# Delta-rule attention and a hardswish MLP in one kernel: two weight-conversion steps change their places in a hand-written order around the first join

## The chip, the cores and the metric

One core of one Trainium2 chip. The metric is the time of one execution of the program on the device, in microseconds, median of several runs. The core has five engines that run side by side, each working through its own queue in order: TensorE (PE in the profile), VectorE (DVE), ScalarE (ACT), GpSimd (POOL) and SyncE (SP, which here issues DMAs). Where one needs what another makes, it waits on a semaphore, and everything behind it in its queue waits too.

## The reference

```python
# q, k, v: (4, 8, 768, 48), beta: (4, 8, 768), all f32
k_n = k / (norm(k, axis=-1) + 1e-6)
for t in range(768):
    y[:, :, t] = q_t @ state
    v_old = state^T k_t
    state = state + beta_t * outer(k_t, v_t - v_old)
x = y.transpose(0, 2, 1, 3).reshape(3072, 384)
h = x @ w_in                              # w_in (384, 2048)
g = h * clip(h + 3, 0, 6) / 6
out = g @ w_out                           # w_out (2048, 384)
```

The weights come in as 64-bit floats, which the kernel turns into 32-bit floats itself.

## The kernel before

**Attention in chunks.** The 768 tokens are cut into 24 chunks t of 32; the four batches lie side by side on the 128 partitions. A chunk needs the inverse X of a 32x32 triangular matrix for each batch and head. Chunk 0 gets it by products on TensorE. Chunks 1 to 4 form the first group: their inverse is a substitution on VectorE for all four at once, with pairs of small operations (L730 product, L735 subtraction), that does both 16x16 halves of each matrix; a memset (L740) and a transpose back (L473) end it. Then each chunk has a *join* that makes the off-diagonal quarter from the two halves: a GpSimd memset, a transpose on VectorE (L694), 64 small products on TensorE (L684, the "first products"), an addition and a second transpose on VectorE (L698, L702), 64 more products (L684, the "second products"), and a ScalarE copy into X (L710).

The chunk's own chain is: products with the state (L806), R on VectorE (two L901, one L909: values less what the state holds), pz = X R on TensorE (L827), the copy Z of it on ScalarE (L927), the output py (L827), the state's update su (L938, applied by L956 on VectorE), and y (L843 on ScalarE, L819 and L863 on VectorE), which TensorE turns (yt, L873) and ScalarE copies to xT (L877).

**The MLP beside it.** Two chunks make a block of 256 tokens. For the very first chunk the up projection runs alone as 16 blocks of w_in columns, f0 to f15, each three accumulated f32 matmuls on TensorE (L994, six PE instructions in the profile). Each is followed by a relu on ScalarE (L1001) and a "second half" on VectorE (L1004) that multiplies it with the PSUM result and thereby frees the PSUM bank. The second chunk has 16 more of its own. These banks come from a ring of four, which the transposes and the products of the attention share. Which result a new one waits for is decided when the program is made: it takes the bank whose last result is read first.

**The weights.** They are 16 pieces, eight of w_in and eight of w_out, numbered from 0. A piece is loaded raw; ScalarE makes its power-of-two scale in four dependent passes over a half-buffer of `spare` (L356, `es[i % 2]`: even pieces use one half, odd pieces the other); VectorE converts in three steps: integer bits of the high word (L378), the low word added (L383), and the product with the scale into its home (L389). The first step and the second go through one common buffer. Column blocks f12 and f13 need piece 6, f14 and f15 piece 7. The program asserts, word by word, that the scale of piece i is begun only after piece i-2 is converted.

**The order.** Up to chunk 5 the order of all this is written out by hand in the string ORDER; a word advances a generator by one step, `*n` n times. The words that matter here:

- `c`: one conversion step (L378, L383, L389 in turn). `a`: one scale pass (L356).
- `i1`: one step of the first group's substitution. `x1`: one step of chunk 1's join. `h1`: one step of chunk 1's chain. `y0`, `y1`: one step of the output of chunk 0 or 1.
- `ua`: one up-projection block of the first chunk (`ub` of the second). `ra`, `rb`: its relu. `ga`, `gb`: its second half.
- `n5`: norms of later keys (a square on ScalarE L407, a reduction on VectorE L413). `k`, `v`, `q`, `w`: DMA issues on SyncE for keys, values, queries and raw weights.

A word gives the engine's queue its next instruction, so the place of a word fixes what stands in front of it on its own engine, and nothing else.

Of the kernel before, what the change touches and what calls it, by code (L numbers as in the profile page):

```python
# [24 lines left out]
n2 k*2 a x0 m2 p1 c*2 p1 n2*3 b1 q b0 s p1 x0 q w x0 n2 q*2 c*3 x0 n4 k p1 k p2*2 x0*2 a*2 c a*2 q*3  # L25
a*2 w v p3*2 q x0 q n4 p2*2 c p2 v c n4*2 a*3 z v n4 c a m3 v c p2 n4*2 q p2 k c b2 h0 c h0 w a*2 h0
p4*2 a*2 m4 p3 q*4 h0 q k w p4*2 c*5 v*2 p3 k p3*3 k*2 p4*2 v*2 p4 m6 k a w a w i1*3 k i1*7 a i1*2 a
i1*2 v i1*2 k b3 k y0 c y0*3 ua*2 ra*2 i1*3 w v ga v a*3 i1*2 ua i1 h1 i1 q w ua ra ua i1 ra*2 ga i1
k ua a*2 ra ga i1 ga ua ra ua ra i1 ga i1*4 ua ga n5 x1*2 k x1 c a ra v a*2 ga x2 k*2 ga*2 ua*2 x1
ra*2 x1*2 ua h1*2 n5 k ga c ra ga*2 h1 c y1*2 ua ra w ga ua ra x2 n5 ga y1*2 ua ra ga h1 v*3 n5*2 k  # L30
y1*2 ua a ra x2 ub*2 a n5 rb*2 h1 x3 ga c*2 v W a h2 y2 gb ub rb gb x2 gb ub*2 n5*2 b4 rb n5 x2*2 h2
gb rb gb m5 a n5*2 y2 ub rb gb v c q*2 v q*5 n5 ub n5 rb gb h2 c h2 q ub y2 h2 y2 rb ub p5 b5 rb
gb*2 a*2 x3 p5 ub y2*2 k p5*2 h2 rb h3 p5 gb h3 ub*2 q rb gb rb gb ub a x3 p6 v c x4 x3 rb gb ub p7
# [1531 lines left out]
```

## Time and profile before

| what | value |
|---|---|
| median of 3 runs | 664.41 us (663.94 to 665.17) |
| the profiled execution | 662.06 us, its span (first to last instruction) 660.3 us |
| TensorE busy | 632.5 us, 96% of the span |
| VectorE busy | 499.2 us, 76% |
| ScalarE busy | 282.3 us, 43% |
| GpSimd busy | 225.1 us, 34% |
| granted TensorE clock, mean | 0.997 of full speed |

Busy shares are means over stages that differ. In the first 60 us the attention is set up, weights stream in, and all engines take turns at holding up the others; later TensorE works nearly without a break. The part that the change touches lies between 53 and 67 us. There, VectorE, ScalarE and TensorE hand work to each other within fractions of a microsecond, so the timelines, which list instructions in order of time, say more than the shares do. In a timeline line the columns are start, length, engine, line of the kernel, operation, output and inputs, shape, count, and in brackets how long the engine had been idle and what ended the wait. A start can overlap the end of the instruction in front of it by about 0.1 us, since an engine takes up the next one while the last drains.

### The profile page before, as it was taken

The numbers are of one execution on the slowest core, as the hardware profiler recorded it, in microseconds if no ns is written. First come the engines' busy times: TensorE is split into PE (matmuls) and PEld (weight loads), VectorE is DVE, ScalarE is ACT, GpSimd is POOL, SyncE is SP. The second block draws the span as 40 slices with busy tenths as digits, with TensorE's granted clock in tenths as the row PEclk, the third lists the DMA queues.
The fourth block names the chain that finished last, engine by engine and source line by source line (L and its number), as shares of the span: only waits on it lengthen the run. The fifth ranks groups of instructions, "written<-read, shape, count | busy, mean of one in ns | idle before, by whom it ended". The sixth has DMA issues, their size and how long they took to land.

```text
span 660.3 us, 26640 instructions
## 1 busy us (share of the span) xinstructions
PE 632.5 (96%) x11640; PEld 569.2 (86%) x11640; DVE 499.2 (76%) x1170; ACT 282.3 (43%) x548; POOL 225.1 (34%) x352
## 2 busy tenths in 40 slices
PE   2768999999999999999999999999999999999997
PEld 2658987776689989999999999999999999999997
DVE  5899877798657988758988848979658998456354
ACT  5887689332243154154154244244244144153250
POOL 6531022003661353553254354164051242331430
PEclk9998999999999999999999999999999999999999
DMA  7888346202040030041030030020020020000000
GB/s 174 204 198 235 77 102 164 51 25 43 9 87 18 3 74 3 3 90 22 3 74 3 2 74 3 2 63 2 3 50 2 3 49 3 23 18 2 26 1 24
DMA packets 88692, 33.28 MB, mean 50 GB/s; under 512 B 80224, under 2 KB 83424, under 8 KB 88576
## 3 DMA queue, kind: packets, MB, share of 16 engines
q1 hardware_dynamic: 88224, 31.29, 20.8%
q8 instruction: 91, 1.49, 0.9%
q10 hardware_dynamic: 352, 0.30, 0.2%
q14 instruction: 25, 0.20, 0.1%
HBM read 26.84 MB, written 4.72 MB: 48 GB/s over the span
## 4 chain that ended last, share of the span: by engine, by line
PE 91%; DVE 3%; DMA 2%; SPq 1%; ACT 1%; issue 1%; DVEq 0%
PE po L1226 28%; PE ph L1066 27%; PE ph L994 9%; PE po L1162 6%; PE ks L806 4%; PE su L938 3%; PE pt L524 3%; PE pz L827 3%; PE py L827 3%; PE sc L547 2%; PE yt L873 1%; DMA spare<-in_moe_w_in_dram 1%; PE pi L684 1%; DMA w_out<-in_moe_w_in_dram 1%; SPq L168 1%
## 5 line engine op out<-in xcount | busy, mean ns | idle before, releaser
L1066 PE MATMUL ph<-xT,w_in 128*128 128x128 f32 (+1 forms) x720 | 156.8, 321 | 0.0
L1030 POOL TENSOR_TENSOR g<-g 128x256 f32<-128x256 f32 (+1 forms) x144 | 88.6, 616 | 104.7 <-ACT g L1080 99.1
L1066 PEld LDWEIGHTS ph<-xT,w_in 128*128 128x128 f32 x720 | 116.8, 191 | 6.7
L1226 PE MATMUL po<-w_out,g 128*128 128x192 f32 x640 | 110.6, 326 | 0.0
L1226 PEld LDWEIGHTS po<-w_out,g 128*128 128x128 f32 x640 | 104.6, 190 | 0.5
L1080 ACT ACTIVATE g<-ph 128x512 f32<-128x512 f32 x72 | 43.1, 598 | 105.1 <-PE ph L1066 105.1
L1226 PE MATMUL po<-spare,g 128*128 128x192 f32 x480 | 86.7, 332 | 0.0
L1226 PEld LDWEIGHTS po<-spare,g 128*128 128x128 f32 x480 | 77.2, 190 | 1.8
L994 PE MATMUL ph<-xT,w_in 128*128 128x128 f32 (+1 forms) x384 | 72.0, 338 | 0.6 <-ACT xT L877 0.6
L1236 POOL TENSOR_TENSOR o<-o,u 128x192 f32<-128x192 f32 x18 | 13.3, 739 | 163.8 <-ACT o L1233 86.6
L994 PEld LDWEIGHTS ph<-xT,w_in 128*128 128x128 f32 x384 | 59.6, 195 | 7.7 <-ACT xT L877 0.8
L1093 DVE TENSOR_TENSOR g<-ph,g 128x256 f32<-128x256 f32 x72 | 30.2, 419 | 46.8 <-PE ph L1066 33.5
L759 DVE TENSOR_TENSOR pr<-A 128x30 f32<-128x30 f32 (+9 forms) x150 | 57.3, 382 | 3.3
L1212 DVE TENSOR_TENSOR g<-g 128x512 f32<-128x512 f32 x80 | 56.1, 722 | 3.5 <-PE po L1226 3.5
L1113 DVE SCALAR_TENSOR_TENSOR g<-o,g 128x512 f32<-128x512 f32 x72 | 52.6, 730 | 7.8 <-ACT o L1110 7.7
L764 DVE TENSOR_TENSOR A<-A,pr 128x30 f32<-128x30 f32 (+9 forms) x150 | 55.1, 367 | 3.3
L1110 ACT ACTIVATE o<-g,halves 128x512 f32<-128x512 f32 x72 | 52.2, 725 | 11.3 <-DVE g L1113 8.4
L1066 PE MATMUL ph<-beta_tok,sums_in 128*128 128x128 f32 x288 | 55.9, 275 | 0.0
L356 ACT ACTIVATE spare<-spare,places 128x768 uint16<-128x768 uint16 (+1 forms) x56 | 52.8, 947 | 3.2 <-DMA kf<-in_k_dram 1.6
L1233 ACT ACTIVATE o<-po 128x192 f32<-128x192 f32 x40 | 13.3, 332 | 82.7 <-PE po L1226 79.2
L510 POOL TENSOR_TENSOR kb<-kf,inv 128x384 f32<-128x384 f32 x24 | 21.7, 907 | 75.5 <-issue 43.1
L1162 PE MATMUL po<-w_out,g 128*128 128x384 f32 x128 | 45.4, 490 | 0.0
(141 smaller groups left out, 1019.1 us busy)
## 6 DMA issues: line engine op xcount, KB each, us to landing
kf<-in_k_dram SPq DMA_DIRECT2D x96, 48.0 KB, 2.6
qb<-in_q_dram SPq DMA_DIRECT2D x96, 48.0 KB, 2.4
vf<-in_v_dram SPq DMA_DIRECT2D x96, 48.0 KB, 2.1
out_dram<-o SPq DMA_DIRECT2D x90, 48.0 KB, 1.6
spare<-in_moe_w_in_dram SPq DMA_DIRECT2D x4, 768.0 KB, 6.6
w_out<-in_moe_w_in_dram SPq DMA_DIRECT2D x4, 768.0 KB, 6.1
w_out<-in_moe_w_out_dram SPq DMA_DIRECT2D x4, 768.0 KB, 5.8
spare<-in_moe_w_out_dram SPq DMA_DIRECT2D x4, 768.0 KB, 5.2
```

Source lines behind the costliest of these rows:

```text
L356: nc.scalar.activation(out=z, in_=z if n else d.bitcast(I16)[:, :, :, 3], func=func, bias=places[:, n : n + 1], scale=scale,)
L759: nc.vector.tensor_tensor(out=pv, in0=A[:, j + 1 :, j].unsqueeze(2).to_broadcast([n, w, j]), in1=A[:, j, 0:j].unsqueeze(1).to_broadcast([n ...
L764: nc.vector.tensor_tensor(out=A[:, j + 1 :, 0:j], in0=A[:, j + 1 :, 0:j], in1=pv, op=ALU.subtract)
L994: nc.tensor.matmul(ph[:, cols], lhsT=w_in[:, s, f * 128 : (f + 1) * 128], rhs=xT[:, s, cols], start=(s == 0), stop=(s == NKT - 1),)
L1030: nc.gpsimd.tensor_tensor(out=out, in0=a, in1=b, op=op)
L1066: nc.tensor.matmul(ph[:, n], lhsT=w, rhs=x, start=start, stop=stop, skip_group_check=True)
L1080: nc.scalar.activation(out=gt, in_=ph[:], func=ACTF.Copy)
L1110: nc.scalar.activation(out=r, in_=g, func=ACTF.Relu, bias=half, scale=1.0 / 6.0)
L1113: nc.vector.scalar_tensor_tensor(out=g, in0=r, scalar=1.0, in1=g, op0=ALU.min, op1=ALU.mult)
L1162: nc.tensor.matmul(pos[c][:], lhsT=gs[blk, f // 2][:, f % 2, c * P : (c + 1) * P], rhs=w_out[:, f, :], start=(f == 0), stop=(f == NFC - 1),)
L1212: nc.vector.tensor_tensor(out=A(f, *out, 4), in0=A(f, *a, 4), in1=A(f, *b, 4), op=op)
L1226: nc.tensor.matmul(ps[n][:], lhsT=A(f - f % 2, *a)[:, f % 2], rhs=b[:, f], start=(f == 0), stop=(f == HF - 1),)
```

## The change

Only ORDER is changed. The same words, in three lines:

```diff
-i1*2 v i1*2 k b3 k y0 c y0*3 ua*2 ra*2 i1*3 w v ga v a*3 i1*2 ua i1 h1 i1 q w ua ra ua i1 ra*2 ga i1
-k ua a*2 ra ga i1 ga ua ra ua ra i1 ga i1*4 ua ga n5 x1*2 k x1 c a ra v a*2 ga x2 k*2 ga*2 ua*2 x1
-ra*2 x1*2 ua h1*2 n5 k ga c ra ga*2 h1 c y1*2 ua ra w ga ua ra x2 n5 ga y1*2 ua ra ga h1 v*3 n5*2 k
+i1*2 v i1*2 k b3 k y0*4 ua*2 ra*2 i1*3 w v ga v a*3 i1*2 ua i1 h1 i1 q w ua ra ua i1 ra*2 ga i1 k ua
+a ra ga i1 ga ua ra ua ra i1 ga i1*4 ua ga n5 x1*2 c a k x1 a ra v a*2 ga x2 k*2 ga*2 ua*2 x1 ra*2
+x1*2 ua h1 c h1 n5 k ga c ra ga*2 h1 c y1*2 ua ra w ga ua ra x2 n5 ga y1*2 ua ra ga h1 v*3 n5*2 k
```

On the engines this is:

- VectorE: piece 6's last conversion step (L389, 128x768) leaves its place inside the substitution (between the L730 and the L735 of 112 elements) and stands directly behind the first join's transpose (L694), where piece 7's first step (L378, 128x768) stood. L378 moves behind R (L901 twice, L909), in front of L413.
- ScalarE: piece 8's first scale pass (L356 reading `w_out`) leaves its place ahead of three relus (f5, f6, f7) and a square (L407), and stands behind them, directly in front of piece 8's second pass and relu f8.
- TensorE, GpSimd and SyncE: the same instructions in the same order.

No instruction is added or taken away, and no buffer is changed.

## The prediction

> **What bounds the kernel now.** I read the page first, then the wait list of TensorE, then busy time by stretch, then the timelines of VectorE, ScalarE and TensorE around the first join. On the page, the chain that ended last is TensorE's nearly throughout. The row by stretch gives (after the stretch and its length) TensorE's busy time: from 61.2 to 600 us it is idle for 0.04 us in all, and in the wait list only one wait is left.
>
> ```profile
> PE 91%; DVE 3%; DMA 2%; SPq 1%; ACT 1%; issue 1%; DVEq 0%
> 61.20:600.00 538.80, 538.76 (x10040) 482.28 (x10040) 421.64 (x984) 219.69 (x443) 188.09 (x273) 1.00 0.17 37
> PE pi L684 <- DVE sums_in L694: 0.9, 1, 0.9
> ```
>
> That wait stands just ahead of 61.2: the first join's first products (L684) wait for its transpose (L694), which ends the substitution on VectorE. So a change here has at most 0.94 us to win, while every microsecond that TensorE is made to wait after 61.2 goes straight into the end. The timelines (start, length, engine, line) show what stands in line:
>
> ```profile
> 53.85 0.95 DVE L389 SCALAR_TENSOR_TENSOR w_in<-spare 128x768 f32<-128x768 f32 x1
> ...
> 58.00 0.28 DVE L1004 SCALAR_TENSOR_TENSOR g<-g,ph 128x128 f32<-128x128 f32 x1
> ...
> 60.74 0.45 DVE L694 STREAM_TRANSPOSE sums_in<-X 128x256 f32<-128x256 f32 x1
> 61.11 0.52 DVE L378 TENSOR_SCALAR spare<-spare 128x768 uint32<-128x768 uint32 x1
> 61.55 0.69 DVE L1004 SCALAR_TENSOR_TENSOR g<-g,ph 128x128 f32<-128x128 f32 x3
> 62.15 0.28 DVE L698 TENSOR_TENSOR sums_in<-pi,corner 128x128 f32<-128x128 f32 x1
> 62.54 0.44 DVE L702 STREAM_TRANSPOSE sums_in<-sums_in 128x256 f32<-128x256 f32 x1
> ```
> ```profile
> 57.54 0.37 ACT L1001 ACTIVATE g<-ph,halves 128x128 f32<-128x128 f32 x1 [0.30 <-PE ph L994]
> 57.81 0.93 ACT L356 ACTIVATE spare<-spare,places 128x768 uint16<-128x768 uint16 x1
> 58.63 1.00 ACT L356 ACTIVATE spare<-w_out,places 128x768 uint16<-128x768 int16 x1
> 59.54 0.88 ACT L1001 ACTIVATE g<-ph,halves 128x128 f32<-128x128 f32 x3
> 60.29 0.53 ACT L407 ACTIVATE sq<-kf 128x384 f32<-128x384 f32 x1
> 60.71 0.94 ACT L356 ACTIVATE spare<-spare,places 128x768 uint16<-128x768 uint16 x1
> 61.53 0.38 ACT L1001 ACTIVATE g<-ph,halves 128x128 f32<-128x128 f32 x1
> ```
> ```profile
> 61.24 0.72 PE L684 MATMUL pi<-X,sums_in 16*32 16x16 f32 x64 [0.94 <-DVE sums_in L694]
> 61.90 1.60 PE L994 MATMUL ph<-xT,w_in 128*128 128x128 f32 x12
> 63.43 0.73 PE L684 MATMUL pi<-X,sums_in 32*32 32x16 f32 x64
> 64.09 0.94 PE L994 MATMUL ph<-xT,w_in 128*128 128x128 f32 x6
> 64.95 0.95 PE L827 MATMUL pz<-R,X 32*32 32x48 f32 x64
> ```
>
> The reader is to see three things: the conversion inside the substitution (53.85); ScalarE's eighth-buffer pass (L356 reading w_out, 58.63), which comes well before the ninth relu (61.53); and VectorE's ninth second half (third of the L1004 at 61.55), which stands in front of L698 and L702, on which TensorE's second products (63.43) depend. I number the relus f0 to f15 by their w_in block; the ninth is f8. Pieces are numbered from 0.
>
> **Step 1, the substitution without the conversion.** It drops 0.87 us of VectorE (the L735 behind it starts at 54.72). But four second halves (L1004) stand in the substitution's queue, and the last, f4, needs the relu that starts at 57.54 and lasts 0.37, so to 57.91; that relu in turn waited 0.30 us for TensorE. With 0.03 us for the signal f4 can start at 57.94 instead of 58.00. Gain 0.06 us; bounds 0 and 0.87. I take 0.06, because the row names the input. L694 then starts at 60.68 and L684 on TensorE at 61.18.
>
> **Step 2, the conversion in its new place.** L389 starts where L378 did, 0.37 behind L694, at 61.05; with its 0.95 it ends at 62.00. L378 had taken 0.52 there.
>
> **Step 3, what that makes late on ScalarE.** The diff also moves one "a" behind the conversion: piece 8's first scale pass (L356 reading w_out). It writes the half-buffer that piece 6's conversion reads (pieces take the two halves by turns), so it cannot start before 62.00. It started at 58.63. ScalarE works in order and behind it stand piece 8's second pass, then relu f8. With 0.04 for the signal: first pass 62.04, its 1.00 and 0.04 to the dependent pass 63.08, 0.82 from there to the relu (60.71 to 61.53) gives 63.90. So relu f8 starts 2.37 late and ends at 64.28 (0.38). The three relus that the pass had preceded come earlier; nothing needs that, since their second halves stand behind the transpose.
>
> **Step 4, from there to TensorE.** VectorE's second half f8 waits until 64.31. Before, the three at 61.55 took 0.69, so the third started at 61.96, L698 0.19 and L702 0.58 after it. Now L698 starts at 64.50 and L702 at 64.89, ending at 65.33; TensorE's second products start at 65.38 instead of 63.43: 1.95 late. TensorE's own cover, blocks f9 and f10 between the two products (1.53 us), is used up by 63.8 even with f9 kept back 0.4 us by its PSUM bank (freed by second half f6, now behind the longer L389). From there it idles 1.6 us.
>
> **Step 5, R and X for pz.** R: L901 starts 0.37 behind L702 (62.91 after 62.54), L909 0.73 later and lasts 0.62, to 66.61. X: relu f8 at 63.90, two passes and two relus in the spacing of before (61.53 to L710 at 64.22 is 2.69), so L710 at 66.59, ending at 66.87. TensorE wants pz at 65.38 + 1.52 = 66.90. Both just make it; bounds 0 to 0.2 us, and I take 0.
>
> **Step 6, L378 behind R.** VectorE reaches the next instruction (L413, before at 64.17) at 64.17 + 2.35 + 0.44 = 66.96, 2.79 late, while TensorE is 1.95 late. What TensorE takes from it next: bank of f9, released 64.90 + 2.79 = 67.69, wanted by f12 at 67.78: in time. Bank of f10, released at 66.2 + 2.79 = 68.99, wanted by f13 at 66.60 + 1.95 = 68.55: 0.45 us late. y (L863 ends 69.11 + 2.79 = 71.90), wanted by yt at 69.86 + 2.40 = 72.26: in time. Piece 7's conversion ends 67.26 + 2.79 = 70.05, wanted by f14 at 70.58: in time. Behind that VectorE had idle time of its own (0.45 at 69.55, 0.64 at 70.94), so its debt falls back to TensorE's.
>
> **Other queues.** SyncE and GpSimd keep their order. GpSimd's memset (L691, 63.04) follows L702 and moves 2.35 us; the state product that needs its bkb stands at 69.05 + 2.40, ample. Value loads follow R by the same 2.4 us and are used much later. No instruction is added, so there is nothing else to pay.
>
> **Sum:** -0.06 + 2.01 (steps 2 to 4) + 0 + 0.45 = **+2.4 us**, kept to the end because TensorE has no wait left to absorb it. The profiled execution took 662.06 us with a span of 660.3, so it would become 664.5. The median of the runs shown is 664.41, 0.35% more; on it the forecast is **666.8 us**.
>
> **Rivals.** *The clock drops too.* These rows give granted clock as the third number from the end:
>
> ```profile
> 45.00:48.40 3.40, 2.32 (x192) 2.09 (x192) 3.37 (x7) 3.33 (x5) 0.47 (x1) 1.00 0.67 191
> 48.50:51.90 3.40, 1.40 (x10) 1.17 (x11) 3.09 (x10) 1.82 (x4) 1.70 (x5) 0.99 1.02 327
> 51.90:55.20 3.30, 3.30 (x37) 3.08 (x40) 3.06 (x10) 2.18 (x4) 0.00 (x0) 0.50 1.04 287
> ```
>
> After 3.4 us with 1.40 busy TensorE ran at half clock for 3.3 us; after 2.32 busy it did not. Mine would have about 1.5 busy in 62.0 to 65.4. If the clock halves, TensorE's work of that stretch costs up to 1.65 us more, but the 0.45 us wait of f13 and some of the other slack vanish in it: about +1.1, 667.9 us. For it: 1.5 is near 1.40. Against: a stretch cut elsewhere holds more work.
>
> [...]
>
> *Faster: the scale pass does not hold relu f8.* If ScalarE could start the pass by about 60.1, relu f8 would come by 62.0 and L702 would lose only the 0.43 us by which L389 is longer than L378; its end at 62.98 has 0.4 us to spare before 63.43. Then the gain of step 1 stays: 0.06 if f4 limits, at most 0.87, so 663.5 to 664.3 us. It decides at relu f8 starting no later than 62.0. Against it: the shared half-buffer.
>
> *Part of it is taken up later*, or relus and passes overlap more tightly: under 1.3 us remain, 665.2 us. Against it: 538.76 of 538.80.
>
> **How the numbers follow.** Forecast 0.58, clock drop 0.22, partly taken up 0.12, faster 0.08. A change within 0.2% (1.3 us) can't be told from none. The forecast and the clock case are slower but for a tail of 0.02: slower 0.78; same 0.14; faster 0.08 (it needs most of 0.87 plus luck, but I leave it whole). The range 665.0 to 668.6 holds the forecast with the bounds of steps 4 to 6, the clock case, and most of the partial one.
>
> **What would show it.** Right: TensorE's list gains a wait of about 1.6 us ahead of the second L684, ScalarE is idle about 1.5 us ahead of the L356 that reads w_out, put down to L389, and VectorE is idle about 2 us ahead of one L1004. Wrong: L356 reading w_out starts before L389 ends, or L694 starts near 59.9, or TensorE shows a new wait of its own before 640 us.

## The result and the profile after

| what | before | after |
|---|---|---|
| median | 664.38 us (22 runs, 661.60 to 667.47) | 666.43 us (22 runs, 665.03 to 670.83) |
| ratio | | 1.0037, 95% interval 1.0025 to 1.0048 |
| profiled execution, span | 662.06 us, 660.3 us | 666.04 us, 664.2 us |

The change makes the kernel slower by 2.05 us on these medians, and by 0.0037 x 664.4 = 2.5 us on the ratio. 666.8 had been forecast. Of the runs further down, two single ones, of 2173.62 us (before) and 1267.26 us (e8), count as slow and are left out of the ratios.

TensorE still carries the chain that ended last. In the windows of after (start and end; length; busy time of TensorE, its weight loads, VectorE, ScalarE, GpSimd; granted clock; DMA share; GB/s) it is no longer free of idle time behind 61.2 us: 538.80 - 536.95 = 1.85 us are idle, where before had 0.04. The list of TensorE's waits from 61 us on names the places (columns: us in total, times, longest):

```profile
61.20:600.00 538.80, 536.95 (x9950) 480.33 (x9950) 419.37 (x979) 218.82 (x440) 188.13 (x273) 0.99 0.17 36
```
```profile
PE pi L684 <- DVE sums_in L702: 0.8, 1, 0.8
PE ph L994 <- issue: 0.5, 1, 0.5
PE ph L994 <- DVE g L1004: 0.3, 1, 0.3
PE py L827 <- issue: 0.3, 1, 0.3
```

The old wait for L694 lies ahead of 61 us and is hardly shorter (0.91 us against 0.94). New against the profile of before are the wait for L702, that for a bank freed by a second half (L1004), and two waits near 100 us for which the profile shows no releaser ("issue"). The last kind isn't the change's own: a second profile of before (e8, below) has waits of 0.6 and 0.2 us without a releaser at 71 and 75 us.

The chain of waits of after (start, length, engine, output, line) shows how the wait for L702 comes about:

```profile
60.02 0.36 DVE sums_in L694
60.38 0.85 DVE w_in L389
61.23 0.02 issue
61.26 0.99 ACT spare L356
62.25 0.02 issue
62.28 0.93 ACT spare L356
63.21 0.26 ACT g L1001
63.48 0.02 issue
63.50 0.29 DVE g L1004
63.79 0.21 DVE sums_in L698
...
64.09 0.46 DVE sums_in L702
64.55 0.04 issue
64.59 1.05 PE pi L684 x64
```

Read from the top: behind the transpose comes the conversion; behind its end comes piece 8's first scale pass on ScalarE; behind that the second pass and relu f8 (L1001); then VectorE's second half f8, L698 and L702, and only then TensorE's second products. The chain leaves VectorE for ScalarE and comes back. In the timelines of ScalarE, VectorE and TensorE the same stretch shows as engines standing idle (the bracket: how long, and for what):

```profile
61.26 0.99 ACT L356 ACTIVATE spare<-w_out,places 128x768 uint16<-128x768 int16 x1 [1.58 <-DVE w_in L389]
```
```profile
63.50 0.29 DVE L1004 SCALAR_TENSOR_TENSOR g<-g,ph 128x128 f32<-128x128 f32 x1 [1.88 <-ACT g L1001]
```
```profile
60.44 0.72 PE L684 MATMUL pi<-X,sums_in 16*32 16x16 f32 x64 [0.91 <-DVE sums_in L694]
61.48 2.28 PE L994 MATMUL ph<-xT,w_in 128*128 128x128 f32 x12 [0.31 <-DVE g L1004]
64.59 1.05 PE L684 MATMUL pi<-X,sums_in 32*32 32x16 f32 x64 [0.83 <-DVE sums_in L702]
...
67.15 1.50 PE L827 MATMUL pz<-R,X 32*32 32x48 f32 x64
```

The same work also takes longer: twelve L994 instructions 2.28 us instead of 1.60, 64 products of L684 1.05 instead of 0.73, pz 1.50 instead of 0.95. The windows show the granted clock at 0.53 and 0.50 there:

```profile
62.00:65.40 3.40, 2.57 (x70) 2.27 (x72) 1.76 (x6) 3.33 (x6) 0.81 (x2) 0.53 0.11 38
68.00:69.00 1.00, 1.00 (x36) 0.88 (x27) 1.00 (x4) 0.28 (x1) 0.00 (x0) 0.50 0.45 86
```

So two of the forecast's cases, the held relu and the clock drop, stand in one profiled execution. The drop begins at 62.2 us, before TensorE stands still for L702 (63.8 to 64.6), so it doesn't follow from that wait. The experiments take the two apart.

### The profile page after: what moved, and what is told of

It reads as the page before. It is cut to its first block, busy times and chain, and to the rows that moved or that the text cites. A ratio compares the mean times of both kernels' runs of the same rounds, so it can differ in the third digit from the quotient of the medians.

```text
span 664.2 us, 26640 instructions
## 1 busy us (share of the span) xinstructions
PE 635.7 (96%) x11640; PEld 571.1 (86%) x11640; DVE 500.1 (75%) x1170; ACT 281.8 (42%) x548; POOL 225.4 (34%) x352
## 4 chain that ended last, share of the span: by engine, by line
PE 91%; DVE 3%; DMA 3%; ACT 1%; SPq 1%; issue 1%; DVEq 0%
PE po L1226 28%; PE ph L1066 27%; PE ph L994 9%; PE po L1162 6%; PE ks L806 4%; PE pt L524 3%; PE su L938 3%; PE pz L827 3%; PE py L827 3%; PE sc L547 3%; PE yt L873 1%; DMA w_out<-in_moe_w_in_dram 1%; ACT spare L356 1%; DMA kf<-in_k_dram 1%; PE pi L684 1%
## 5 line engine op out<-in xcount | busy, mean ns | idle before, releaser
L1226 PE MATMUL po<-w_out,g 128*128 128x192 f32 x640 | 110.6, 326 | 0.0
L1226 PEld LDWEIGHTS po<-w_out,g 128*128 128x128 f32 x640 | 104.6, 190 | 0.5
L1226 PE MATMUL po<-spare,g 128*128 128x192 f32 x480 | 86.7, 332 | 0.0
L1226 PEld LDWEIGHTS po<-spare,g 128*128 128x128 f32 x480 | 77.2, 190 | 1.8
L994 PE MATMUL ph<-xT,w_in 128*128 128x128 f32 (+1 forms) x384 | 72.8, 339 | 2.2 <-DVE g L1004 1.1
L994 PEld LDWEIGHTS ph<-xT,w_in 128*128 128x128 f32 x384 | 59.9, 195 | 9.9 <-DVE g L1004 1.6
L356 ACT ACTIVATE spare<-spare,places 128x768 uint16<-128x768 uint16 (+1 forms) x56 | 52.5, 942 | 2.6 <-DMA kf<-in_k_dram 1.4
L1162 PE MATMUL po<-w_out,g 128*128 128x384 f32 x128 | 45.4, 490 | 0.0
```

What stands on the lines that cost most here:

```text
L356: nc.scalar.activation(out=z, in_=z if n else d.bitcast(I16)[:, :, :, 3], func=func, bias=places[:, n : n + 1], scale=scale,)
L994: nc.tensor.matmul(ph[:, cols], lhsT=w_in[:, s, f * 128 : (f + 1) * 128], rhs=xT[:, s, cols], start=(s == 0), stop=(s == NKT - 1),)
L1162: nc.tensor.matmul(pos[c][:], lhsT=gs[blk, f // 2][:, f % 2, c * P : (c + 1) * P], rhs=w_out[:, f, :], start=(f == 0), stop=(f == NFC - 1),)
L1226: nc.tensor.matmul(ps[n][:], lhsT=A(f - f % 2, *a)[:, f % 2], rhs=b[:, f], start=(f == 0), stop=(f == HF - 1),)
```

## The experiments

Each kernel was timed in rounds against the kernel before on the same chip. Medians of before were 663.32 (33 runs), 663.55 (35) and 663.37 us (18) in the three sets; ratios are with a 95% interval. To compare traces I measure from the start of the substitution (A, the first L469), so that nothing earlier counts: to L694, from there to L702, from the first to the second products, from these to pz, from pz to the state's update su, and A to su in all. The last column is read from the granted clock in windows of 0.1 us. In the edits shown, each line has only the words around the place.

| kernel | A to L694 | to L702 | products 1 to 2 | to pz | pz to su | A to su | half clock after 45 us |
|---|---|---|---|---|---|---|---|
| before | 13.04 | 1.80 | 2.19 | 1.52 | 4.10 | 21.35 | 51.8 to 55.2 |
| before again (e8) | 13.02 | 1.77 | 2.19 | 1.53 | 4.25 | 21.47 | until 46.9 |
| after | 12.27 | 4.14 | 4.15 | 2.56 | 4.85 | 24.32 | 62.2 to 69.0 |
| after again (e4) | 12.60 | 4.17 | 4.17 | 1.52 | 4.79 | 23.58 | until 47.0, 50.4 to 53.9 |
| e1 | 12.26 | 2.17 | 2.82 | 2.56 | 5.71 | 23.84 | until 46.4, 63.5 to 70.3 |
| e2 | 13.14 | 2.32 | 2.33 | 1.52 | 4.24 | 21.72 | until 54.3 |
| e3 | 13.03 | 1.68 | 2.19 | 1.52 | 4.29 | 21.52 | 50.6 to 54.1 |
| e5 | 12.41 | 2.37 | 3.82 | 1.78 | 4.02 | 22.52 | 52.2 to 55.6, 62.4 to 65.8 |
| e6 | 12.85 | 4.17 | 4.18 | 1.52 | 4.24 | 23.28 | 50.2 to 53.6 |
| e7 | 12.92 | 2.18 | 2.19 | 1.52 | 4.24 | 21.37 | 50.7 to 54.1 |
| e9 | 13.04 | 4.16 | 4.16 | 1.52 | 4.79 | 24.01 | until 45.9, 52.7 to 56.1 |
| e10 | 12.29 | 2.17 | 2.19 | 1.52 | 4.24 | 20.72 | until 48.9 |
| e11 | 13.03 | 1.78 | 2.19 | 1.53 | 4.02 | 21.26 | until 49.6 |
| e12 | 12.93 | 2.36 | 2.57 | 1.53 | 4.60 | 22.11 | until 45.9, 52.8 to 56.2 |

**The kernels before and after, once more.** They give a second trace of each, and a control of the timing.

> The changed kernel once more, for a second profile and more times. Hold theory: ratio 1.0025 to 1.0048 as before; ScalarE idle 1.4 to 2.4 us ahead of the pass that reads w_out until L389 ends, VectorE idle about 2 us ahead of second half f8, whatever the clock does. Clock theory (the loss is the half clock that follows the gap): in a profile without half clock between 60 and 70 us, TensorE's start of the state product (L938) after the first pz is no later than in the kernel before, and the loss stands only in profiles that show half clock there.

> The kernel before once more, for a second profile. Hold theory: ratio 0.999 to 1.001, and the distance from the substitution's first transpose (L469) to the first join's transpose (L694) is 12.9 to 13.0 us, against 12.1 to 12.6 in the changed kernel, depending on when relus f2 to f4 end.

After again: 665.84 us, ratio 1.0041 (1.0025 to 1.0058). Before again: 663.66 us, 1.0007 (0.9989 to 1.0024). This trace of after has no half clock behind 54 us, so the hold can be read in it alone. The timelines of TensorE, ScalarE and VectorE in it:

```profile
61.09 0.73 PE L684 MATMUL pi<-X,sums_in 16*32 16x16 f32 x64 [1.25 <-DVE sums_in L694]
62.12 1.60 PE L994 MATMUL ph<-xT,w_in 128*128 128x128 f32 x12 [0.31 <-DVE g L1004]
65.26 0.73 PE L684 MATMUL pi<-X,sums_in 32*32 32x16 f32 x64 [1.53 <-DVE sums_in L702]
...
67.96 2.00 PE L994 MATMUL ph<-xT,w_in 128*128 128x128 f32 x12 [0.30 <-DVE g L1004]
```
```profile
61.91 1.01 ACT L356 ACTIVATE spare<-w_out,places 128x768 uint16<-128x768 int16 x1 [1.92 <-DVE w_in L389]
```
```profile
64.17 0.29 DVE L1004 SCALAR_TENSOR_TENSOR g<-g,ph 128x128 f32<-128x128 f32 x1 [1.90 <-ACT g L1001]
```

With the products at full length (0.73, 1.60) and the granted clock at 1.00 from 57.2 us on, TensorE's wait ahead of the second products is 1.53 us. The hold needs no slower clock.

**One step of the change undone: the passes (e1).** The changed kernel, with piece 8's four scale passes behind relus f8 to f13:

```diff
-n5 x1*2 c a k x1 a ra v a*2 ga x2
+n5 x1*2 c k x1 ra v ga x2
-ra x2 n5 ga y1*2 ua ra ga h1
+ra x2 n5 a ga y1*2 ua ra a ga h1
-h2 y2 rb ub p5 b5
+h2 y2 rb a*2 ub p5 b5
```

> The changed kernel, with piece 8's four scale passes taken out from in front of relu f8 and of X and put behind the square that follows f13 and later relus (piece 9's last two move on in turn). VectorE and TensorE keep the changed kernel's order. Hold theory (the 2 us come from piece 8's passes, which wait for the moved conversion and hold up relu f8 and X): ScalarE's wait for L389 and VectorE's wait of 1.9 us for relu f8 are gone, the second products start within 2.3 us of the first, and what the substitution gave stays: 0.99935 to 1.0007 times the kernel before (-0.45 to +0.45 us, the gain of 0.06 to 0.87 less the bank of f13). L378 theory (L378 behind R makes banks late, and the passes matter little): about as slow as the changed kernel, +1.5 us or more, ratio 1.0023 or more.

663.91 us, ratio 1.0013 (0.9996 to 1.0030), no longer told from before and 1.9 us below the changed kernel (e4) in the same set; the ratio lies above the 1.0007 that the hold theory allowed and below the 1.0023 of its rival. L702 comes 2.17 us behind L694 instead of 4.14 to 4.17: the hold is gone. Its trace has the clock at half from 63.5 to 70.3 us, which is why its stretch from the first to the second products (2.82) and those behind it are long all the same.

**One step alone: the pass (e2) and L378 (e3).** Both start from the kernel before and leave L389 in the substitution. e2 moves piece 8's first pass to where the change has it, e3 moves L378 behind R:

```diff
-k ua a*2 ra ga i1
-n5 x1*2 k x1 c a ra
+k ua a ra ga i1
+n5 x1*2 k x1 c a*2 ra
```
```diff
-k x1 c a ra
-ua h1*2 n5 k ga c
+k x1 a ra
+ua h1 c h1 n5 k ga c
```

> The kernel before with only piece 8's first scale pass moved to where the changed kernel has it; all conversions stay where they were, so the pass has nothing to wait for. Hold theory: the pass starts right after the square, some 0.6 us later than 60, relu f8 comes about 0.9 us late, of which 0.4 us is slack ahead of the second products: +0.4 us (0 to +0.9), ratio 1.0000 to 1.0014. Order theory (the late place of the pass alone makes the cost, not the wait for the conversion): +1.5 to +2.5 us, ratio 1.0023 to 1.0038.

> The kernel before with only piece 7's first step (L378) moved behind R; the conversion stays inside the substitution and all passes where they were. Hold theory: VectorE's work ahead of the second products shrinks by 0.44 us where it had 0.4 us of slack, and behind R it is where it was: no change, -0.2 to +0.2 us, ratio 0.9997 to 1.0003. L378 theory: banks and y come late and it is slower by 0.5 us or more, ratio 1.0008 or more.

663.32 us, ratio 1.0008 (0.9991 to 1.0026), and 663.58 us, 0.9999 (0.9979 to 1.0019). With the conversion done long before, the pass has nothing to wait for in its new place, and A to su grows by 0.25 to 0.37 us; 0.14 us of it lies between the first and the second products, where the two passes now stand together ahead of relu f8. L378 behind R costs nothing that is seen. Neither move alone is the cost; it takes the late conversion and the pass that waits for it together.

**The shared half-buffer (e5).** The changed kernel, with a half-buffer of its own for piece 8, so that the pass no longer waits for L389 while every queue keeps its order:

```diff
-            d, z = raws[i], like(es[i % 2], i)
+            d, z = raws[i], like(es_of(i), i)
...
+    def es_of(i):
+        return own16 if i == 8 else es[i % 2]
```

> The changed kernel with a half-buffer of its own for piece 8's scale (in the output tile o, which is not in use yet), so that its first pass no longer waits for the moved conversion. Every engine's order is that of the changed kernel. Hold theory: ScalarE's wait of 1.6 to 1.9 us ahead of the pass goes, relu f8 starts 1.2 to 1.9 us sooner after L694 than in the changed kernel, VectorE's wait for it falls under 0.7 us and TensorE's wait for L702 under 0.5 us; 1.0000 to 1.0018 times the kernel before, at least 1 us faster than the changed kernel. Order theory (the passes' place on ScalarE costs it, whoever they wait for): as slow as the changed kernel, ratio 1.0030 or more.

664.81 us, ratio 1.0026 (1.0009 to 1.0042): between what the two theories had asked for, so the time alone settles nothing. The trace does. ScalarE's and VectorE's timelines:

```profile
60.34 0.98 ACT L356 ACTIVATE o<-w_out,places 128x768 uint16<-128x768 int16 x1
...
62.19 0.35 ACT L1001 ACTIVATE g<-ph,halves 128x128 f32<-128x128 f32 x1
```
```profile
61.15 0.92 DVE L389 SCALAR_TENSOR_TENSOR w_in<-spare 128x768 f32<-128x768 f32 x1
61.99 0.87 DVE L1004 SCALAR_TENSOR_TENSOR g<-g,ph 128x128 f32<-128x128 f32 x3
62.77 0.28 DVE L698 TENSOR_TENSOR sums_in<-pi,corner 128x128 f32<-128x128 f32 x1
```

The pass starts before L389 does, and neither engine waits: the brackets of 1.6 to 1.9 us are gone. L702 stands 2.37 us behind L694. Of the 4.17 - 1.80 = 2.37 us that the change adds there, the shared buffer makes 1.80 and the order 0.57, of which the longer L389 in L378's place is the larger part (the next instruction starts 0.84 behind it, 61.15 to 61.99; behind L378 it was 0.44, 61.11 to 61.55). That the time did not come down as far agrees with the clock of its trace: half from 62.4 to 65.8 us. How often that happens in the timed runs isn't known, so this part stays open.

**L378 put back ahead of the products (e6).** The changed kernel, with L378 directly behind L389:

```diff
-n5 x1*2 c a k x1
+n5 x1*2 c*2 a k x1
-ua h1 c h1 n5
+ua h1*2 n5
```

> The changed kernel with L378 left ahead of the first join's second transpose, directly behind the moved conversion, instead of behind R. Hold theory: its 0.44 us hides in VectorE's wait of 1.9 us for relu f8 and no longer stands ahead of second halves f9 and f10; f13's wait for its bank (0.3 us in a profile without half clock) goes, and nothing else: 0.2 to 0.5 us less than the changed kernel, ratio 1.0018 to 1.0042, and a distance from the first join's transpose to the state product that is 0.2 to 0.5 us shorter. L378 theory (L378 behind R is the main loss): ratio 1.0015 or less.

664.47 us, ratio 1.0023 (1.0007 to 1.0038); the interval overlaps that of after again. In the trace the stretch from pz to su falls from 4.79 to 4.24 us, as short as in before, and the bank wait behind pz is gone. The hold stays (4.18 from the first to the second products), and f9's wait for its bank grows from 0.31 to 0.91 us within it. So L378 behind R does cost about half a microsecond in the changed order, where everything behind it is late already, though it costs nothing in before's order (e3).

**Everything out of the way (e7).** The changed kernel with second half f6 ahead of L389, the passes late as in e1, and piece 7's three steps together behind the second halves (the lines for the first two late passes are those of e1):

```diff
-n5 x1*2 c a k x1 a ra v a*2 ga x2
+n5 x1*2 ga c k x1 ra v x2
-ua h1 c h1 n5 k ga c ra ga*2 h1 c y1*2
+ua h1*2 n5 k ga ra ga*2 h1 c*3 y1*2
-h2 y2 rb ub p5 b5
+h2 y2 rb a*2 ub p5 b5
```

> A version meant to keep only the gain: the conversion behind the first join's transpose but behind second half f6, piece 8's passes behind relus f8 to f13, and piece 7's three steps together behind the second halves of f9 to f11. Hold theory: TensorE has no wait between the first join's first products and the state product beyond 0.2 us, and what the substitution gave stays where the relu of f4 lets it: ratio 0.9985 to 1.0003. Clock theory (a gap of 0.9 us ahead of the first products and small ones behind it are enough for the half clock, which eats the gain): ratio 1.0000 to 1.0020, with half clock between 60 and 72 us in its profile.

663.15 us, ratio 1.0001 (0.9983 to 1.0019). From L694 on TensorE runs as in before, and A to su is the same too, 21.37 us. It isn't faster: of the substitution's 0.87 us only 0.12 arrived in this trace (12.92 us from A to L694), and TensorE's wait for the first transpose is as long as ever:

```profile
59.93 0.73 PE L684 MATMUL pi<-X,sums_in 16*32 16x16 f32 x64 [0.98 <-DVE sums_in L694]
60.58 1.60 PE L994 MATMUL ph<-xT,w_in 128*128 128x128 f32 x12
62.12 0.72 PE L684 MATMUL pi<-X,sums_in 32*32 32x16 f32 x64
```

**Keeping TensorE busy through the join (e9 to e12).** To see what the clock costs, a few f32 products of 128x128 were added into unused columns of an older bank: three ahead of the first products in all four kernels (0.89 us together in each trace), and five more ahead of the second products in e9 (1.28 us). e9 is the changed kernel, e10 is e7, e11 the kernel before, e12 is e5.

```diff
+    def filler():
+        while True:
+            nc.tensor.matmul(
+                banks_of[-2][:, P:TB], lhsT=w_in[:, 0, 0:128], rhs=xTs[0][:, 0, 0:P],
+                start=True, stop=True, skip_group_check=True,
+            )
+            yield
```

> The changed kernel with extra products whose results nobody reads: three ahead of the first join's first products and five ahead of its second (0.26 us each), so that TensorE is busy in its gaps there; nothing else waits for them longer than before. Hold theory by itself: no change against the changed kernel, ratio 1.0030 to 1.0045. Clock theory (a part of the loss is the half clock that follows the gaps in some executions): no half clock between 58 and 72 us in the profile, and 0.5 us or more less than the changed kernel, ratio 1.0010 to 1.0030.

> The version with everything moved (e7_all_moved), with three such products ahead of the first join's first products. Hold theory by itself: as e7_all_moved, ratio 0.9990 to 1.0010. Clock theory: no half clock behind the gap in any execution and the substitution's gain stays, ratio 0.9983 to 0.9997.

> The kernel before with the same three products ahead of the first join's first products. The two profiles of the kernel before show no half clock behind that gap, so both theories say no change, ratio 0.9990 to 1.0010; if it gains 0.7 us or more (0.9990 or less), the gap costs the kernel before too.

> The changed kernel with piece 8's own half-buffer (e5_third_buffer) and the three products ahead of the first join's first products. If what e5_third_buffer kept of the loss (ratio 1.0026, half clock from 62.8 to 66.2 us in its profile) is the half clock: ratio 0.9995 to 1.0013 and no half clock there. If it is the passes' place ahead of relu f8 and X: ratio 1.0020 or more, with TensorE waiting for L702 or pz.

The first three missed every range; e12's time lies in that of its slower theory, but without the waits for L702 or pz that belonged to it. The ratios are 1.0115 (1.0091 to 1.0139), 1.0052 (1.0035 to 1.0069), 1.0054 (1.0035 to 1.0072) and 1.0055 (1.0033 to 1.0077). The cost doesn't lie at the join: e10 has the shortest A to su of all, 20.72 us, and e11 is no longer there than before. In e10, e11 and e12 TensorE stands some 40 us later for 2.0 to 2.3 us ahead of the same instruction, with no releaser in the trace (TensorE's timeline, first e10, then e11; L1172 is L1162 of the unfilled kernels). In e9 such waits come at other lines, 2.0, 1.4 and 0.7 us in its list.

```profile
100.80 1.45 PE L1172 MATMUL po<-w_out,g 128*128 128x384 f32 x4 [2.34 <-issue]
```
```profile
102.04 1.45 PE L1172 MATMUL po<-w_out,g 128*128 128x384 f32 x4 [2.00 <-issue]
```

So the filled kernels' times say nothing on the clock, and in all four the releaser of these waits stays unknown. What remains of use is the table: none of the four was at half clock between 58 and 72 us, though e9's wait for L702 and e12's delay were there, so no run was had with the filler and the drop together.

## Why the forecast held, step by step

The clean trace of after (e4) is set against before, the places named as in the forecast.

- **Step 1, the substitution without the conversion: the mis-sized term.** 0.06 us was taken, within 0 to 0.87; e4 shows 13.04 - 12.60 = 0.44, the profile of after 0.77, e6 0.19, e7 0.12. "L694 starts near 59.9", one of the forecast's own signs of being wrong, did come in the profile of after (59.95). The table says why. Where the conversion is out of the substitution and TensorE was at full clock from 50 us to the transpose, A to L694 is 12.26 to 12.29 us (after, e1, e10), a gain of 0.75 to 0.78. Where it was at half clock for one stretch around 50 to 56 us, blocks f2 to f4 and their relus came late, and the second halves inside the substitution's queue took back between 0.1 and all of it (e4, e5, e6, e7, e9, e12: 12.41 to 13.04); in all of these but e5 VectorE is seen to wait 0.25 to 0.55 us for such a relu, and in after, e1 and e10 it isn't. The profile of before happened to have that stretch, and I read the relu that it shows as the kernel's limit; it was that execution's. With the conversion in place the length is 13.02 to 13.14 in either case (e8 and e11 without the half clock, before, e2 and e3 with it), so it hides the difference. (The forecast also counted four second halves in the substitution behind L389; there are five, f0 to f4, with f4 the last as it said.)
- **Steps 2 to 4, the hold: right in mechanism and size.** The forecast was that relu f8 starts 2.37 us late with L694 0.06 early, 2.43 against L694; in e4 it starts 3.20 us behind L694 (63.79 - 60.59), in before 0.79 (61.53 - 60.74): 2.41. In after it is 3.17. The second products were to come 2.01 us later against the first; measured 4.17 - 2.19 = 1.98. TensorE's wait was to be 1.6 us; it is 1.53 in e4. e1 and e5 each remove it, one by taking the pass out of the way and one by taking the buffer.
- **Step 5, R and X in time for pz: right.** 1.52 us from the second products to pz in e4, as in before.
- **Step 6, f13's bank: right in kind, too small.** In e4 block f12, forecast to be in time, already waits 0.30 us for its bank, and f13 starts 3.77 us behind the second products (69.03 - 65.26) instead of 3.17 (66.60 - 63.43), so 0.60 late against 0.45. pz to su grew by 0.69 us in all (0.54 against e8). The step took 0.44 us for L378, from its start to the next start in the old place; behind R it holds VectorE for 0.77 us (66.40 to 67.17). There it runs beside GpSimd's L486, and both are longer: L378 takes 0.85 to 0.86 us in the seven traces where they overlap (after, e1, e3, e4, e5, e9, e12), against 0.52 to 0.56 in the seven where they don't; the two L486 take 1.51 us in after against 1.19 in before, and GpSimd's four instructions there, of which they are the last, 2.46 to 2.47 in those seven against 2.15 in before, e2, e6, e7 and e8. With L378 put ahead (e6) the wait is gone and the stretch is 4.24 us.
- **The sum.** A to su grew by 23.58 - 21.35 = 2.23 us (2.11 against e8), as -0.44 + 1.98 + 0 + 0.69. The total fits partly by luck: the errors of step 1 (0.38 too little gain) and step 6 (0.24 too little loss) have opposite signs. The ratio's 2.5 us lies 0.3 higher, inside its interval (1.7 to 3.2 us).
- **The rival "the clock drops too": a drop happened, but not always, and not behind the new wait.** The profiled execution of after has it from 62.2 us on, ahead of the wait for L702; e4, with the longer wait (1.53 us), and e6 have none there. From e4 to after, A to su grows by 0.74 us although the substitution is 0.33 shorter, so the two windows cost 1.07 us there; 1.1 had been worked out for one. The mean granted clock over all runs is 0.983 for the changed kernel (10 runs of e4) and 0.981 (22 runs of the result), against 0.986 for before (32 runs), with a scatter of 0.005 to 0.009 between runs. That leans towards the changed kernel meeting it more often but doesn't show it, since it counts half clock anywhere in the program, and the clocks of before in the set of the result aren't on record.
- **The rivals "faster" and "taken up later": refuted.** The pass started at 61.26, not by 60.1, and held by the half-buffer. "Taken up later" allowed less than 1.3 us in the end; the ratio's interval begins at 1.7. The traces alone wouldn't decide it: from su to the last group of products (L1226) it is 585.1 us in before and 586.9 in e8, 586.1 in after and 585.4 in e4, so two executions of one kernel differ there by more than the two kernels do. The two "issue" waits of after, 0.74 us in all, are a new wait before 640 us, another of the forecast's signs of being wrong; e8 has such waits too.

The gain that the move could have had shows in e10's trace, 0.75 us up to L694 and 0.63 up to su, and in no time: e7, which keeps nothing of the hold, measures 1.0001. No kernel here beat the one before.

## What to carry to other kernels

When an instruction is moved in one engine's queue, look up who writes next into what it reads: here a scale pass on ScalarE waited 1.6 to 1.9 us for the old reader of its buffer, and the relu behind it, which needed neither, carried that delay to VectorE and TensorE. A limit read from one execution may be that execution's clock: here the gain was put at 0.06 us, and the traces at full clock from 50 us to the transpose showed 0.75 to 0.78. Before a gain is set to nothing because "the other engine isn't ready", check whether that engine was at full speed there.

## What the runs showed of the hardware

**Behind 45 us the half clock came in stretches of 3.4 us or twice that, at other places in each execution.** Of those that begin there, nine last 3.4 to 3.5 us (before, e3, e4, two in e5, e6, e7, e9, e12) and two 6.8 (after, e1). An earlier one is longer: e4 shows 0.50 from 36.7 to 46.9 us. The same kernel had one at 62.2 to 69.0 us once (after) and at 50.4 to 53.9 the other time (e4). In after it followed TensorE waits of 0.91 and 0.31 us.

**The busy time of the stretch before, taken by itself, doesn't decide it.** In after, half clock followed 3.4 us with 2.18 us of TensorE busy (58.8 to 62.2 us), in before 3.4 us with 1.30 (48.4 to 51.8). Full clock followed 3.4 us with 1.76 us busy in e6 (60.5 to 63.9) and 1.48 in e8 (47.1 to 50.5). So the forecast's comparison of 1.40 with 2.32 was no rule. What decides it stays open.

**VectorE and GpSimd both take longer in one pair.** L378 beside L486 takes 0.85 to 0.86 us instead of 0.52 to 0.56, in seven traces against seven, and the two L486 take 1.51 in after instead of 1.19 in before (step 6). An instruction moved to another place can so have another price. No run moved L486 itself.

**A few added products came with waits far from where they stand.** With three more products, 0.89 us in all and partly in a gap, TensorE waited 2.0 to 2.3 us without a releaser near 100 us in three different kernels (e10, e11, e12). In the kernels without them the longest such wait is 0.6 us (e8). The cause wasn't found. The fillers weren't free in this program (ratios of 1.0052 to 1.0115), and their own rows didn't give the price.
